# Maxout of the last three chunks as seven products of quarters, and a new order table

## The chip, the cores and the metric

The program runs on one core of a Trainium2 chip. The metric is the device time in microseconds (us) of one execution; lower is better. The engines are TensorE (PE in the profile, its weight loads PEld), VectorE (DVE), ScalarE (ACT), GpSimd (POOL) and SyncE (SP, which only issues DMAs here).

## What is computed

Linear attention with an exponential feature map over 8 batches of 8 heads, 576 positions and 64 channels, then a feed-forward layer whose hidden value is the maximum of three products (maxout):

```python
def phi(x):
    proj = np.einsum('bhsd,df->bhsf', x, w_phi)
    proj = proj - np.max(np.abs(proj), axis=-1, keepdims=True)
    return np.concatenate([np.exp(proj), np.exp(-proj)], axis=-1)
q_p, k_p = (phi(q), phi(k))
kv = np.einsum('bhsf,bhsd->bhfd', k_p, v)
z = np.sum(k_p, axis=2)
num = np.einsum('bhsf,bhfd->bhsd', q_p, kv)
den = np.einsum('bhsf,bhf->bhs', q_p, z)[..., None] + 1e-06
attn_out = num / den
x = attn_out.transpose(0, 2, 1, 3).reshape(B * S, H * D)      # 4608 x 512
h = np.maximum(np.maximum(x @ w1, x @ w2), x @ w3)            # 4608 x 768
out = h @ w_out                                               # 4608 x 512
```

## The kernel before

**Attention in 16 units.** A unit is half a batch: four heads. Its k and q come by DMAs on POOL's queue (nodes Lk and Lq, lines 431 and 421) into one of four slots `qk_bf` in bf16, its v by SP (Lv, into one of four slots `raw`). The channel-major copy `qkT` is made on PE for the first four units and by transposing DMAs of SP (T, line 516) for the others. PE projects (G, into `psk`, `pst`, `psq`; M, into `psm`), DVE takes the maxima (line 538), ACT the exponentials `Ek` and `Eq` (lines 542 and 622), POOL scales v into `vab` (line 586), PE sums `kvps` (K, line 605) and multiplies the numerators `psn` (N, line 672), DVE combines two halves into `y` (lines 681, 684) with a reciprocal (line 729), POOL divides (line 730), and a transposing DMA (X, line 762) puts the result into `xT`, four tiles of 128 channels by tokens.

**Feed-forward in nine chunks of 512 tokens.** Chunks 0 to 7 are the first 512 positions of a batch each; chunk 8 is the last 64 positions of all batches, gathered by POOL (C, lines 1044 and 1045). The maximum is taken relative to the first product: w2 and w3 are replaced by the differences w2−w1 and w3−w1 (line 976, six POOL instructions), and w1·w_out is one matrix, `line_w`. A chunk is then

out = x·(w1·w_out) + max(0, x·(w2−w1), x·(w3−w1))·w_out.

Per chunk PE makes 12 products of 128 hidden rows by 512 tokens (`up` and `up2`, line 880, four matmuls of 512 columns each into a PSUM bank `ups`). ACT or DVE cuts the first at zero into `hT` (lines 894, 896), DVE takes the maximum with the second (line 890). Then, for four tiles of 128 tokens, PE adds x·(w1·w_out) (`straight`, line 913) and hT·w_out (`down`, line 918) in one bank; ACT or DVE copies it (osb, line 928) and SP stores it.

**The order is a table.** The nodes are built in a fixed sequence and numbered; the text `PLAN` lists them again in the order in which they are emitted. A word such as `471G@74.8` is node 471 on engine G (T is PE, D is DVE, A is ACT, G is POOL, S is SP); digits before the @ are the slots or PSUM banks that it opens. Each engine does its nodes in that order and waits by semaphores for what a node needs. The number behind the @ orders nothing; the kernel only uses it in `fill`, which puts matmuls on a constant tile (`idler`, line 1060) where PE is expected to be free in the first 30 us.

**What is already there for the change.** `seven_products` and a block that makes `w_sums` exist before, but the set `SEVEN` of the chunks that use them is empty. For a pair jp of hidden blocks, with the chunk's x cut into quarters (halves of its tokens by halves of its channels) and both differences cut into halves of their channels, seven products of 256 tokens (`product`, each two blocks of two matmuls of 256 columns) give what eight give directly. They need sums of x quarters (`sums`, node xs, four per chunk) and of weight quarters (`w_sums`, node ws, four per pair). Behind each chain of products stand additions of a PSUM bank to a part in SBUF (`joined`, node uj, seven per pair, DVE), one copy (us, ACT), two cuts at zero (hr, ACT) and two maxima (hx, DVE). These temporaries take slots of others: `w_sums` all four of `qk_bf`, `sums` one of `qkT`, the parts two of `raw` per pair.

Of the kernel before, what the change touches and what calls it, by code (L numbers as in the profile page):

```python
# [55 lines left out]
SEVEN = ()  # L56
# [34 lines left out]
10S0@0.7 103G0@1.2 3S@1.1 1D@0.8 4A@1.1 5D@4.1 11A1@3.9 12D@4.3 0G@1.9 19T0@4.7 20D0@5.2 6A@4.2 29T12@5.6 34A0@6.1 32D0@6.1 33A0@6.5  # L91
9G@2.5 16S0@1.7 106T3@6.1 107D1@6.8 112T45@7.5 35D@7.3 119T67@7.7 31A@7.0 30A@7.5 8G@3.2 25T0@8.2 115D1@8.0 125D@8.6 116A1@8.0
117A1@8.5 7D@9.2 26D@9.3 102G@3.9 259G2@4.6 1166G@5.3 2G@6.1 186G3@6.3 17G@9.1 13S@3.1 118D@9.7 23T3@10.2 51T21@10.6 73T05@10.8
260G@9.3 104G@10.1 1169G@10.3 15D@10.3 14D@10.5 52D0@11.0 53D@11.6 27T2@11.8 28D@12.2 114A@8.9 120A@9.4 113A@9.9 121A@10.4 122D@12.4
76A0@11.2 124A@11.7 74A@12.2 77A0@12.7 21T1@12.4 43T24@12.7 110T6@13.2 22D@13.0 46D@13.3 75A@13.1 36T51@13.5 24D@13.7 47D@14.0
334S1@3.5 18S1@4.9 39D@14.3 108T0@13.8 185G@11.0 111D@14.9 48T34@14.5 42D@15.1 1167G@11.8 45A@13.8 54A0@14.1 44A@14.3 123A@14.6
38A@15.1 37A@15.6 56G0@14.5 55G@15.6 49D@15.7 109D@16.3 68T62@15.3 69A@16.1 58A@16.5 60G@16.9 105S2@5.6 126T75@16.2 50D@16.9 130D1@17.5
129D@17.9 57G@18.0 61G@18.1 59G@18.3 40A@16.7 70A@17.2 402G1@19.4 71A@17.7 41A@18.2 72A@18.7 134T30@17.1 136D@18.2 135D@18.8 62T45@18.3
78T6@18.9 137A1@19.1 81A0@19.3 79A@19.5 128A@19.8 131T12@19.3 64D0@19.4 63D@19.6 132D@19.8 187S0@10.4 80A@20.1 65T03@19.6 66D@20.4
151T54@20.1 82T16@20.6 67A@20.3 127A@20.5 141A@20.7 133D@20.6 90T03@20.9 83D0@21.2 155A1@20.9 154A1@21.4 91D1@21.6 85T72@21.4 86D@22.0  # L100
84D@22.4 92D@22.8 153A@21.9 1178T1@21.8 1180T4@22.2 93T07@22.7 1176T6@23.0 1179A0@22.4 152A@23.3 1181D@23.2 87D@23.8 161T3@23.4
138G1@20.1 190T1@23.5 162A@23.8 163A@24.1 191A2@24.3 1177D@24.2 94D@24.7 140G@21.2 142G@21.3 261G@22.4 139G@22.6 143G@23.7 1168G@24.8
144G@25.6 145T54@24.1 156T23@24.7 164A1@25.2 147A1@25.4 158A@25.6 157A@26.0 160A@26.5 88D0@25.1 95D@25.3 267T1@25.4 268D3@25.7
146D@25.9 265T6@25.5 148T04@26.1 404G@25.7 89G0@25.9 188G@27.1 96D1@26.1 97G@27.4 333G0@28.6 335G@29.3 337S0@40.7 332G@29.5 266D@26.2
165T27@26.7 168T15@27.1 150A@27.0 159A@27.1 149A@27.6 166D2@27.3 169D@27.7 194T6@27.5 263T4@27.6 167D@28.1 195A@27.9 173T30@28.1
196T21@28.5 170D@28.5 264A@28.3 176T76@28.9 174D0@28.9 171D2@29.3 177D@29.4 178D@30.0 175D@30.4 1186T5@29.2 200A0@29.2 201A0@29.7
198A@30.2 1187A@30.7 202D0@30.8 179D0@31.4 403G@30.3 172G1@31.0 203T43@30.6 276T76@30.8 180G@32.2 205A@31.1 208A@31.6 197A@32.1
280A1@32.6 281A1@33.0 207A@33.5 1172G@33.6 1170G@35.7 100T0@31.1 101D@31.6 279D1@32.0 192T5@31.4 189S3@42.1 193D@32.6 1184T1@31.9
1188T0@33.1 199D@33.2 282D@33.8 1185A@34.0 204A@34.5 283T52@34.5 262S0@42.8 181T6@34.7 1182T1@35.0 209D@34.4 287D0@35.0 206D@35.3
1171G@37.8 182D@35.9 1183D@36.5 277A@35.0 284A@35.4 1189A@35.7 278A@36.2 285A@36.6 183T3@36.3 301T24@36.7 184D@37.1 338S@43.5  # L110
473S0@45.0 405S1@46.9 336S2@47.6 1173G@39.9 1175G@42.0 98T6@37.0 99D@37.5 288T10@37.4 269T73@37.7 286D@37.9 290D@38.3 1202T6@38.1
302A0@37.1 304A@37.6 273A@38.1 751S1@48.2 303A0@38.6 305A@39.1 271A@39.6 1203A1@40.0 289D@38.9 291T50@39.0 406S1@49.6 274A@40.5
270A@41.0 1192T2@39.4 292D@39.5 293D@40.1 1193D@40.7 1198T4@40.2 1199D@41.3 210T61@41.2 213D@41.9 214D1@42.2 275D@42.6 228T50@41.3
1194T2@41.6 231A1@41.7 230A1@42.2 1195A@42.7 232A@43.2 1204T4@42.5 272D@43.2 1205D@43.8 1206T1@43.4 229A@43.6 306T32@44.3 218T07@44.5
1207D@44.4 219D@45.0 220D@45.6 215T45@44.8 1214T1@45.2 216D@46.2 1215D@46.8 1200T0@46.1 238T7@46.9 211A@44.1 221A0@44.4 309A@44.8
1196T4@47.0 310A@45.2 212A@45.7 294A1@46.0 308A@46.2 314A0@46.6 239A@47.2 307A@47.5 240A@48.0 217D@47.4 1201D@48.0 1174G@44.1
222G0@46.5 339T12@48.0 353T63@48.2 233T75@48.4 1197A@48.2 297A1@48.7 224A@48.8 357D0@48.6 223G@48.5 1212T0@48.8 356D0@49.0 345D@49.3
225T43@50.5 1213D@49.9 342D@50.5 236A@48.9 237A@49.4 234A@49.9 235A@50.4 241A1@50.9 295G@50.6 344A0@51.8 227D0@51.8 296G@52.7 226A@52.3
354A0@52.6 355A@52.8 343A@53.1 346T05@51.6 1210T7@51.9 242T34@52.8 407S@52.8 1208T6@53.2 541G2@54.7 352D@52.2 349D@52.8 243D1@53.4
1211D@53.8 752G3@55.4 472G0@55.7 749G@56.4 542G@57.1 351A@53.6 245T23@54.1 350A@54.0 341A@54.5 364A0@55.0 340A@55.2 298T75@54.7  # L120
244D@54.4 246D@54.8 1209D@55.2 415T14@55.8 247D@55.8 299A1@56.0 300A@56.3 348A@56.6 347A@57.0 418D1@56.3 250T26@56.2 253T37@56.5
1228T5@56.8 311T0@57.7 251D2@56.9 1216T2@57.8 254D@57.3 420A1@57.5 252D@57.7 255D@58.1 421D@58.5 365G0@57.8 313A@58.0 312A@58.2
# [170 lines left out]
def kernel(  # L293
# [798 lines left out]
```

## Time and profile before

| | |
|---|---|
| median of 3 timed runs | 283.32 us (283.1 to 283.32) |
| the profiled execution | 285.92 us, of it 284.1 us span |
| granted PE clock, mean | 0.988 |
| busy: PE, DVE, ACT, POOL | 269.6, 216.4, 200.8, 161.9 us |
| chain that ended last | PE 81%, DMA 7%, ACT 5%, DVE 3%, issue 2% |
| up matmuls (line 880) in that chain | 28% |

The span runs from the first to the last instruction; the execution's time has the launch around it as well. A row of the profile reads: line, engine, operation, output<-inputs with their shapes, count, then busy us and the mean duration of one in ns, then the idle time of that engine just before these instructions and what ended it. Matmul durations overlap, so how fast they follow each other is read from several in a row. The chain of work that ended last lists start, duration and what ran. In the table of stretches the busy us of each engine stand with the number of its instructions.

### The profile page before, as it was taken

The numbers are of one execution on the slowest core, as the hardware profiler recorded it, in microseconds if no ns is written. First come the engines' busy times: TensorE is split into PE (matmuls) and PEld (weight loads), VectorE is DVE, ScalarE is ACT, GpSimd is POOL, SyncE is SP. The second block draws the span as 40 slices with busy tenths as digits, with TensorE's granted clock in tenths as the row PEclk, the third lists the DMA queues.
The fourth block names the chain that finished last, engine by engine and source line by source line (L and its number), as shares of the span: only waits on it lengthen the run. The fifth ranks groups of instructions, "written<-read, shape, count | busy, mean of one in ns | idle before, by whom it ended". The sixth has DMA issues, their size and how long they took to land.

```text
span 284.1 us, 8392 instructions
## 1 busy us (share of the span) xinstructions
PE 269.6 (95%) x3399; PEld 151.8 (53%) x3438; DVE 216.4 (76%) x444; ACT 200.8 (71%) x482; POOL 161.9 (57%) x166
## 2 busy tenths in 40 slices
PE   6879999999996999999999999999999999999993
PEld 4647754576553465546654546555556654444442
DVE  2799999999895788999898898788997871055410
ACT  4599999999995789679889888689699320321011
POOL 8559999998496773462939716576764071000000
PEclk9799999999998999999999999999999999999999
DMA  7999999999999699999999697693027007040054
GB/s 135 244 229 205 208 187 253 260 194 187 224 144 193 129 236 145 218 229 189 254 186 181 143 196 163 160 211 60 3 77 131 2 3 200 2 178 6 3 140 155
DMA packets 76214, 44.52 MB, mean 157 GB/s; under 512 B 52688, under 2 KB 67344, under 8 KB 76176
## 3 DMA queue, kind: packets, MB, share of 16 engines
q1 hardware_dynamic: 61184, 32.19, 51.8%
q0 software_dynamic: 14912, 11.77, 27.9%
q8 instruction: 27, 0.44, 0.6%
q14 instruction: 11, 0.09, 0.1%
q10 hardware_dynamic: 80, 0.03, 0.0%
HBM read 34.64 MB, written 9.44 MB: 155 GB/s over the span
## 4 chain that ended last, share of the span: by engine, by line
PE 81%; DMA 7%; ACT 5%; DVE 3%; issue 2%; POOL 0%; POOLq 0%; ACTq 0%; DVEq 0%
PE ups L880 28%; PE ops L918 16%; PE ops L913 11%; PE psn L672 6%; PE kvps L605 6%; PE psk L534 3%; ACT Eq L622 2%; PE psm L631 2%; DMA qkT<-qk_bf 2%; PE psq L534 2%; DMA qk_bf<-in_q_dram 2%; DMA qk_bf<-in_k_dram 2%; PE pm L1012 2%; ACT Ek L542 1%; PE tps L497 1%
## 5 line engine op out<-in xcount | busy, mean ns | idle before, releaser
L880 PE MATMUL ups<-xT,w_bf 128*128 128x512 bf16 x415 | 101.6, 381 | 1.2 <-issue 0.2
L622 ACT ACTIVATE Eq<-psm 128x512 bf16<-128x512 f32 (+1 forms) x160 | 80.4, 575 | 11.4 <-PE psm L631 7.6
L586 POOL TENSOR_TENSOR vab<-v_raw,em 128x1152 bf16<-128x1152 f32 (+1 forms) x36 | 68.3, 1905 | 26.3 <-ACT em L580 25.1
L542 ACT ACTIVATE Ek<-psk 128x512 bf16<-128x512 f32 x128 | 71.4, 629 | 6.0 <-PE psk L534 5.0
L880 PEld LDWEIGHTS <-w_bf 128*128 128x128 bf16 x432 | 39.5, 98 | 43.5 <-issue 1.8
L730 POOL TENSOR_TENSOR x_sb<-y,rden 128x640 bf16<-128x640 f32 x32 | 39.8, 1254 | 35.8 <-DVE rden L729 28.5
L894 ACT ACTIVATE hT<-ups 128x512 bf16<-128x512 f32 x40 | 24.0, 611 | 37.9 <-PE ups L880 37.9
L918 PE MATMUL ops<-wout_bf,hT 128*128 128x512 bf16 (+2 forms) x215 | 50.2, 373 | 0.5 <-issue 0.2
L538 DVE TENSOR_REDUCE mk<-psk 128x4 f32<-128x512 f32 x64 | 42.8, 682 | 4.0 <-PE psk L534 2.3
L538 DVE TENSOR_REDUCE mq<-psq 128x4 f32<-128x512 f32 x64 | 41.5, 682 | 3.2 <-PE psq L534 3.0
L890 DVE TENSOR_TENSOR hT<-hT,ups 128x512 bf16<-128x512 bf16 x54 | 35.6, 675 | 9.9 <-PE ups L880 7.1
L681 DVE TENSOR_TENSOR y<-psn,sq 128x325 f32<-128x325 f32 x64 | 30.5, 490 | 9.9 <-PE psn L672 9.5
L918 PEld LDWEIGHTS <-hT 128*128 128x128 bf16 x222 | 20.6, 98 | 22.4 <-issue 0.2
L672 PEld LDWEIGHTS <-Eq 128*128 128x128 bf16 x640 | 26.4, 98 | 11.3 <-issue 0.9
L684 DVE TENSOR_TENSOR y<-y,psn 128x325 f32<-128x325 f32 x64 | 30.0, 487 | 2.4 <-DVE y L681 0.5
L672 PE MATMUL psn<-kv_sb,Eq 128*128 128x65 bf16 x640 | 28.8, 194 | 0.0
L928 ACT COPY osb<-ops 128x512 f32<-128x512 f32 (+2 forms) x25 | 14.6, 586 | 17.7 <-PE ops L918 13.1
L534 PEld LDWEIGHTS <-qkT 64*128 64x128 bf16 x576 | 18.4, 95 | 14.7 <-issue 10.9
L913 PE MATMUL ops<-xT 128*128 128x512 bf16 x85 | 24.2, 381 | 0.6
L605 PE MATMUL kvps<-vab,Ek 64*128 64x65 bf16 x1152 | 22.2, 191 | 0.2 <-POOL vab L590 0.2
L605 PEld LDWEIGHTS <-Ek 64*128 64x128 bf16 x1152 | 20.6, 94 | 2.3 <-DVE mk L538 0.4
L913 PEld LDWEIGHTS <-xT 128*128 128x128 bf16 x128 | 11.2, 98 | 12.7 <-issue 1.3
(68 smaller groups left out, 259.6 us busy)
## 6 DMA issues: line engine op xcount, KB each, us to landing
v_raw<-in_v_dram SPq DMA_DIRECT2D x16, 576.0 KB, 5.7
out_dram<-osb SPq DMA_DIRECT2D x32, 256.0 KB, 2.7
qk_bf<-in_k_dram POOLq DMA_DIRECT2D x15, 288.0 KB, 8.4
qk_bf<-in_q_dram POOLq DMA_DIRECT2D x15, 256.0 KB, 8.2
w_bf<-in_moe_w_dram POOLq DMA_DIRECT2D x3, 768.0 KB, 16.7
tail_raw<-in_q_dram SPq DMA_DIRECT2D x16, 64.0 KB, 5.6
wout_bf<-in_moe_w_out_dram POOLq DMA_DIRECT2D x1, 768.0 KB, 19.5
out_dram<-osb SPq DMA_DIRECT2D x6, 128.0 KB, 2.3
```

The lines of the kernel that those rows point to most:

```text
L534: nc.tensor.matmul(ps[s]()[:, i, :], lhsT=qkT()[r, n, :], rhs=wph[r, :], start=True, stop=True)
L538: return nd(kind, {"DVE": 0.598 if n == 4 else 0.331}, lambda: nc.vector.tensor_reduce(dst(m()), ps()[:, 0:n, :], AXX, ALU.max, apply_abso ...
L542: return nd("ek", {"ACT": 0.478 if n == 4 else 0.264}, lambda: nc.scalar.activation(dst(Ek[g]()), ps()[:, 0:n, :], EXP, scale=1.0 - 2.0 * ...
L586: made.append(chosen(n_, lambda n_, g=g, t0=t0, t1=t1: (nc.vector if n_.eng == "DVE" else nc.gpsimd).tensor_tensor(vab()[:, g, t0:t1, 0:D] ...
L605: nc.tensor.matmul(kvps[ab]()[:, pr, g, :], lhsT=Ek[g]()[r, t, :], rhs=vab()[r, g, t, :], start=(pr == prs[0] and g + j == 0), stop=(pr == ...
L622: return nd("eq", {"ACT": 0.478 if n == 4 else 0.264}, lambda: nc.scalar.activation(Eq[g]()[:, t0:t0 + n, :], ps()[:, 0:n, :], EXP, scale= ...
L672: nc.tensor.matmul(psn[g]()[:, i, :], lhsT=Eq[g]()[:, t, :], rhs=kv()[:, pr, ab, g, :], start=True, stop=True)
L730: divs[pr] = nd("x", {"POOL": 1.2}, lambda pr=pr, y=y, rden=rden: nc.gpsimd.tensor_tensor(x_sb()[:, pr].rearrange("p t a d -> p a t d"), y ...
L880: nc.tensor.matmul(ups()[:, o * n:(o + 1) * n], lhsT=w_bf[i + (not plain)][:, ct, jj * P:(jj + 1) * P], rhs=tokens_of(ct)[:, cols] if halv ...
L890: nc.vector.tensor_tensor(dst, dst, src, ALU.max)
L913: nc.tensor.matmul(ops_()[:, 0:hi - lo], lhsT=tile_of(ct, tt), rhs=line_w[c_i > MOVE][:, ct, lo:hi], start=(ct == 0), stop=False)
L918: nc.tensor.matmul(ops_()[:, 0:hi - lo], lhsT=hT()[:, j, tt * P:(tt + 1) * P], rhs=wout_bf[:, j, lo:hi], start=plain and j == 0, stop=(j = ...
```

## The change

Two edits in the code and a new table:

- `SEVEN` becomes chunks 6, 7 and 8: they use `seven_products` in place of 12 full products.
- The weight sums (ws) may stand on POOL only; before, DVE was named too. They did not exist in the program before, since `SEVEN` was empty.
- `PLAN` is replaced as a whole. It was laid out against five sets of measured DMA landings. With 1688 nodes instead of 1565, numbers from 1176 on are other nodes than before.

```diff
-SEVEN = ()
+SEVEN = (6, 7, 8)
...
 PLAN = """
-10S0@0.7 103G0@1.2 3S@1.1 1D@0.8 4A@1.1 5D@4.1 11A1@3.9 12D@4.3 0G@1.9 19T0@4.7 20D0@5.2 6A@4.2 29T12@5.6 34A0@6.1 32D0@6.1 33A0@6.5
...
+1560D@264.7 1668T@263.2 1669A0@264.7 1579D@265.0 1595T@264.5 1674S@258.6 1678S@261.9 1583T@265.8 1587T@267.1 1670S@265.4 1596D3@266.1
+1597S@266.8 1584A1@267.3 1588A2@268.6 1590T2@268.4 1591T@269.3 1585S@268.0 1589S@269.3 1592A0@270.8 1593S@271.4
...
-                got.append(chosen(node("ws", 0, {"DVE": 0.35, "POOL": 1.05}, None, need, used + [w_tiles[i]], port=True), minus_))
+                got.append(chosen(node("ws", 0, {"POOL": 1.05}, None, need, used + [w_tiles[i]], port=True), minus_))
```

The table has 11 more lines, so behind it a line of the kernel before, say 880, is line 891 after. What changes in the program, counted: PE has 288 up matmuls of 512 columns instead of 432, and 252 of 256 columns; DVE has 63 uj, 18 hx and 2 xs more, 18 maxima, 7 cuts at zero and 3 output copies less; ACT has 9 us and 18 hr more and 11 cuts less; POOL has 12 ws and 10 xs more. There are 63 idle matmuls instead of 48.

**POOL's queue at the loads of units 6 and 7.** L431 is a k load, L421 a q load, L586 and L590 make `vab`, L730 divides, L468 casts a piece of q's last positions. Before, the k load of unit 6 is followed by the q load of unit 10, then comes this stretch, from the k load of unit 7 to the q load of unit 6:

```order
L431 DMA qk_bf<-in_k_dram 128x2x576
L586 TENSOR_TENSOR vab<-v_raw,em 128x18x64
L590 CAST vab<-em 128x36
L468 CAST qk_bf<-tail_raw 128x2x64
L730 TENSOR_TENSOR x_sb<-y,rden 128x2x5x64
L586 TENSOR_TENSOR vab<-v_raw,em 128x18x64
L730 TENSOR_TENSOR x_sb<-y,rden 128x2x5x64
L468 CAST qk_bf<-tail_raw 128x2x64
L730 TENSOR_TENSOR x_sb<-y,rden 128x2x5x64 x2
L586 TENSOR_TENSOR vab<-v_raw,em 128x18x64
L590 CAST vab<-em 128x36
L421 DMA qk_bf<-in_q_dram 128x4x256
```

After (lines 11 higher), from the `vab` of unit 3 on: the k load of unit 6, the q loads of units 6 and 7, a division, the k load of unit 7:

```order
L597 TENSOR_TENSOR vab<-v_raw,em 128x18x64 x2
L442 DMA qk_bf<-in_k_dram 128x2x576
L432 DMA qk_bf<-in_q_dram 128x4x256 x2
L741 TENSOR_TENSOR x_sb<-y,rden 128x2x5x64
L442 DMA qk_bf<-in_k_dram 128x2x576
L601 CAST vab<-em 128x36
```

Unit 6's q load moved from behind its k load by twelve rows to directly behind it; unit 10's q load moved to a later place.

**DVE near the program's end.** Before, with `hT<-hT,ups` the maximum of the second product, `hT<-ups` the first cut at zero and `osb<-ops` an output copy, the last rows are:

```order
L890 TENSOR_TENSOR hT<-hT,ups 128x512 x3
L928 COPY osb<-ops 128x512
L896 TENSOR_SCALAR hT<-ups 128x512 x2
L890 TENSOR_TENSOR hT<-hT,ups 128x512
L896 TENSOR_SCALAR hT<-ups 128x512
L890 TENSOR_TENSOR hT<-hT,ups 128x512
L928 COPY osb<-ops 128x512
L896 TENSOR_SCALAR hT<-ups 128x512
L890 TENSOR_TENSOR hT<-hT,ups 128x512 x10
L928 COPY osb<-ops 128x512 x4
```

After, L829 is a join (uj), L864 an hx, L799 a sum of x quarters. A piece from the middle of the joins, where chunk 6 ends and chunks 7 and 8 begin:

```order
L829 TENSOR_TENSOR parts<-ups,parts 128x512 x3
L829 TENSOR_TENSOR hT<-ups,parts 128x2x256 x2
L829 TENSOR_TENSOR parts<-ups,parts 128x512
L829 TENSOR_TENSOR hT<-ups,parts 128x16x32
L799 TENSOR_TENSOR sums<-xT 128x512
L864 TENSOR_TENSOR hT<-hT,parts 128x2x256 x2
L829 TENSOR_TENSOR parts<-ups,parts 128x512 x3
L829 TENSOR_TENSOR hT<-ups,parts 128x16x32
L829 TENSOR_TENSOR parts<-ups,parts 128x512 x4
L864 TENSOR_TENSOR hT<-hT,parts 128x16x32 x2
```

DVE's last 27 instructions, behind its last reciprocal, become 80: 58 joins, 18 hx, one sum and three output copies.

**PE behind the last numerators.** Before, 120 matmuls of `ups` of 512 columns stand behind the last `psn`; after, 224 of 256 columns, with eight more of `straight` and six more of `down` (512 columns) that stood ahead of it. The last ten of all are, before, the 128 last columns of chunk 8, and after, a `straight` and a `down` of 512 columns of chunk 7.

More of the change, by code (lines that the diff above doesn't have):

```diff
@@ L95 @@
[L95 to L122, printed above, removed]
@@ new lines @@
+122D@10.6 26D@11.2 15D@11.5 117A@10.6 23T2@11.4 18S1@4.9 123A@11.1 116A@11.5 120A@12.0 24A@12.5 124A@13.0 1166G@11.0 188G@11.8
+1169G@12.0 51T10@11.8 115D@11.7 52D0@12.3 27T3@12.1 28D@12.9 14D@13.1 73T56@12.6 53D@13.3 74A0@13.4 105S2@5.6 1167G@12.7 75A0@13.9
+76A@14.4 77A@14.9 21T2@13.5 22D@13.9 43T74@13.8 48T13@13.9 46D@14.3 49D@14.6 47D@15.2 50D@15.5 54A0@15.3 68T05@14.6 36T62@15.5
+126T14@15.7 70A@15.6 44A@16.0 45A@16.3 69A@16.6 71A@17.0 72A@17.5 129D@16.1 42D@16.5 41A@18.0 333G1@13.9 334S0@9.0 108T3@16.3
@@ new lines @@
+1110T41@195.4 1117T57@195.6 1019D0@194.9 1020D@195.5 1405A@195.5 1115A@196.0 1412T2@195.8 1061G0@195.0 1060G@197.0 1416T3@196.7
+1420T0@197.5 1113D@195.9 1121D0@196.5 1116D@196.8 1120D@197.4 1417D@197.8 1111A@196.7 1062A@197.1 1413A@197.2 1118A@197.9 1119A@198.2
+1128A1@198.4 1129G1@199.1 1112A@198.6 1114A@199.1 1418T7@198.4 1021T32@199.2 1131G@201.2 1108A@199.6 1391S@182.0 1421D@198.6
+1424T5@199.6 1076T4@200.4 1078A0@200.7 1010T10@200.5 1022D@199.8 1419D@200.2 957S@193.3 1403S@195.1 1023D@200.8 1440T3@200.8
@@ new lines @@
+1011D@201.2 1107A@201.0 1071T72@201.8 1125T16@202.0 1024D0@201.6 1012D@201.8 1425D@202.2 1016D1@202.8 1441T@202.3 1436T0@203.7
+1025G1@201.9 1126D@202.9 1127D@203.5 1017G@203.1 1077A1@201.5 1072A@202.2 1074A@202.7 1075A@203.2 1073A@203.7 1442A3@204.2
+1122T51@204.6 1135T64@204.8 1053T27@205.1 1137A1@205.3 1136A0@205.7 1124D@205.1 1123D@205.6 1054D@206.2 1055D@206.8 1139A@206.2
+1399S@195.7 1138A@206.7 1145T3@205.3 1437T@205.5 1130G@204.3 1056T61@206.9 1146A@207.2 1602G@206.3 1026S@204.4 1132T52@207.1
@@ new lines @@
+1151D@212.7 1093D@213.1 1083T36@214.2 1472D@213.5 1470D1@214.1 1080T75@214.5 1450T4@214.8 1144A@213.4 1143A@213.9 1142A@214.4
+1141A@214.9 1433T@215.3 1160T01@216.6 1187G@213.9 1443S@205.9 1084D2@214.7 1155D2@215.1 1156G2@215.4 1081D@215.2 1085D@215.6
+1082D@216.0 1451D@216.4 1452T3@216.9 1486T7@217.3 1157T65@217.7 1094D0@217.0 1086D1@217.2 1161D1@217.3 1095G0@217.3 1604G@218.5
+1456T4@218.1 1434A0@216.8 1463A@217.2 1453D@217.7 1158D@218.3 1490T0@218.5 1459T2@218.9 1162D@218.7 1159D@219.1 1435S@217.4
@@ new lines @@
+1524G@236.5 1623T2@236.2 1530D@236.5 1624D@237.1 1535D0@237.7 1619D@238.3 1506T@236.7 1531T0@238.0 1527T5@238.4 1626D@238.9 1514T@238.8
+1515A1@240.3 1628D@239.2 1532D@239.6 1536T2@240.1 1528D1@240.3 1537D@240.9 1635T1@240.6 1629T3@241.0 1538T0@241.4 1534D@241.6
+1539D@242.2 1633T5@241.9 1631T2@242.3 1630A2@241.6 1634D@242.8 1632D@243.3 1636D3@243.9 1640T6@242.7 1637T0@243.2 1639D@244.5
+1648T3@243.6 1652T5@244.1 1650T2@244.5 1507A0@242.1 1644A@244.1 1540A@244.6 1649A0@245.1 1638D@245.1 1641D@245.7 1642T1@244.9
@@ new lines @@
+1659T4@245.3 1654T3@245.8 1671T0@246.2 1563T6@247.1 1653D@246.3 1643D@246.9 1646A@246.5 1564A3@247.7 1647D@247.5 1645D@247.9
+1655D2@248.2 1651D@248.8 1519A2@248.2 1520S@248.9 1660D@249.4 1665A@250.2 1663A@250.7 1667T5@247.5 1569T1@248.4 1656T6@248.8
+1661T3@249.2 1571T2@249.7 1582T7@250.1 1544T4@251.0 1658D@250.0 1657D@250.6 1662D@251.2 1664D@252.0 1666D@252.3 1567T6@251.4
+1679T3@252.0 1545A2@252.0 1565T4@252.6 1672T@253.1 1516S@249.5 1431S@250.1 1568D@252.7 1573D0@253.5 1570D@254.1 1542A@252.5 1543D@254.7
@@ new lines @@
+1566D@255.0 1680T@254.4 1578A@255.8 1681D2@255.6 1683T6@255.3 1548T1@255.6 1550T4@256.0 1684T@256.4 1673A1@256.2 1682S@256.2
+1508S@257.4 1572D@256.1 1541D@256.7 1594T3@256.8 1549D@257.0 1685D3@257.6 1686S@258.0 1551D1@257.8 1574T0@257.6 1552T2@258.1
+1546T1@258.5 1575D@258.4 1580A@259.2 1675T6@258.9 1676T@259.8 1557T4@261.1 1555T0@261.5 1687A@259.6 1677A2@261.3 1554D@259.0
+1547D@259.6 1553D@260.4 1556D@262.2 1561A@262.9 1559A@263.4 1558D@262.8 1581D@263.4 1562D@263.7 1586T6@261.9 1576T1@262.8 1577D@264.1
```

228 lines of the change are left out of this document (119 added, 109 removed).

## The prediction

> **What bounds the kernel now.** I read the engines' shares over the span first, then a table of five stretches, then the chain that ended last, and last the one wait in it that is not TensorE's.
>
> ```profile
> span 284.1 us, 8392 instructions
> ...
> PE   6879999999996999999999999999999999999993
> ...
> DVE  2799999999895788999898898788997871055410
> ACT  4599999999995789679889888689699320321011
> ...
> PEclk9799999999998999999999999999999999999999
> ```
>
> TensorE (PE) is full from the fourth slice to the end but for slice 13; VectorE (DVE) is nearly as full up to slice 32 and then half idle. The same by stretches (columns after the times: busy us of PE, PEld, DVE, ACT, POOL, then granted clock, DMA share, GB/s):
>
> ```profile
> 15.00:75.00 60.00, 58.09 (x969) 36.24 (x977) 58.92 (x128) 58.60 (x153) 52.77 (x49) 1.00 1.17 210
> 75.00:100.00 25.00, 22.04 (x275) 11.51 (x278) 18.89 (x40) 19.62 (x47) 20.37 (x22) 0.93 0.97 180
> 100.00:225.00 125.00, 123.68 (x1798) 70.42 (x1814) 108.49 (x222) 104.73 (x253) 72.58 (x67) 1.00 0.82 157
> 229.00:279.00 50.00, 49.74 (x231) 22.95 (x235) 19.78 (x33) 8.25 (x15) 4.73 (x6) 1.00 0.30 86
> ```
>
> Up to 75 us three engines share the limit. From 100 us PE sets the pace (1.3 us of 125 idle), and from 229 us it does so alone: DVE has 30.2 us of 50 free. The one hole is in 75 to 100, where PE has 3 us without work at a clock of 0.93. The chain there, and PE's own rows:
>
> ```profile
> 77.24 6.55 DMA qk_bf<-in_q_dram
> ...
> 83.81 6.95 DMA qkT<-qk_bf
> ...
> 90.80 0.61 PE psm L631
> ```
> ```profile
> 90.80 0.61 PE L631 MATMUL psm<-qkT,wph 64*128 64x512 bf16 x2 [2.64 <-DMA qkT<-qk_bf]
> ```
> ```profile
> 88.00:90.80 2.80, 0.17 (x6) 0.04 (x2) 1.06 (x2) 0.60 (x2) 0.68 (x1) 0.91 1.30 238
> 90.80:94.20 3.40, 3.18 (x18) 1.58 (x20) 1.21 (x3) 2.07 (x4) 3.29 (x4) 0.57 0.93 180
> ```
>
> GpSimd issues unit 6's q load at 77.24, it lands at 83.79, SyncE's transpose of it lands at 90.76, and PE waits 2.64 us. Then the clock is 0.57 for 3.4 us: at full clock its 3.4 us would have been 1.94, so 1.46 us more. **The stall costs 4.1 us in this execution.** The Trainium skill, "TensorE: Matmul & The Clock Gate", section "HAM oscillation — how this bites in real kernels", has only idle gaps above about 3.4 us throttle the clock; the 2.64 us here was followed by the low clock, so the trace does not agree.
>
> The sum starts from this execution's 285.92 us (span 284.1 and 1.8 outside it). The timed runs' median is 283.32, 2.6 less. PE's other rows are back to back, so I put that difference on the stall (my inference): about 1.5 of its 4.1 us is in the median.
>
> **The seven products: −3.5 us of PE.** The pitch of matmuls comes from the chain, where they stand back to back:
>
> ```profile
> 34.46 0.45 PE tps L497 x8
> ...
> 142.86 1.73 PE ups L880 x8
> ...
> 228.28 0.62 PE psn L672 x20
> 229.17 4.05 PE ups L880 x18
> ...
> 279.53 0.35 PE ops L918 x6
> ```
>
> 512 columns: 1.73/8 = 0.2163 us; 128 columns: 0.45/8 = 0.0562. On the line through both, 256 columns take 0.1096. Each of the three chunks gives up 48 matmuls of 512 (2 differences, 6 blocks, 4 channel tiles) for 84 of 256 (3 pairs, 7 products, 4 matmuls). That is 144 × 0.2163 = 31.1 us out, 252 × 0.1096 = 27.6 in: **−3.5**. Were 256 columns exactly half of 512, it would be −3.9; that end goes into the range. Weight loads double per column but are hidden beside matmuls (PEld 23 of 50 us).
>
> **Where it falls.** Behind the last psn matmul (numerators of the last unit) before has by the order 120 up matmuls and the rest of the down and straight ones, 51.1 us at these pitches; the chain has 228.90 to 279.88, 51.0. After, 224 of 256 columns (24.6 us), 120 of 512 (26.0), 10 of 384 (1.6) and 10 of 128 (0.6) stand there: 52.7. So 1.6 us more lies behind it, and 3.5 + 1.6 = 5.1 us less ahead. The attention ahead must then run 5.1 us tighter on DVE and ScalarE (ACT), which are 87% and 84% busy at 100 to 225. What PE loses in such company: 1% there now, 3.2% at 15 to 75 with both at 98%. On 125 us the range is 0 to 4.0 us more; I take **+1.4**, a loss twice today's, since the nearer row is this stretch's own.
>
> **Can DVE carry the joins?** It gets 63 joins (uj, a product in PSUM plus a part in SBUF), 18 hx (maximum of two bf16 halves in SBUF) and 2 of the token sums, and loses 18 maxima (L890), 7 of the first copies (L896) and three output copies on balance.
>
> ```profile
> L538 DVE TENSOR_REDUCE mk<-psk 128x4 f32<-128x512 f32 x64 | 42.8, 682 | 4.0 <-PE psk L534 2.3 <-ACT Ek L542 1.6
> ...
> L890 DVE TENSOR_TENSOR hT<-hT,ups 128x512 bf16<-128x512 bf16 x54 | 35.6, 675 | 9.9 <-PE ups L880 7.1 <-ACT hT L894 2.2 <-ACT sq L650 0.2
> ...
> L896 DVE TENSOR_SCALAR hT<-ups 128x512 bf16<-128x512 f32 x14 | 9.5, 685 | 10.7 <-PE ups L880 10.7
> ...
> L453 DVE CAST qk_bf<-k_raw 128x256 bf16<-128x256 f32 x1 | 0.3, 286 | 0.0
> ```
> ```profile
> 41.26 2.40 DVE mq L538 x4
> ```
>
> A DVE row of 512 values out of PSUM lasts 0.68 but its successor starts 0.60 after it (2.40/4). So a join is 0.60, or 0.68 where it is held until the one before is through. An hx has no row. It is at most the 0.60 of a PSUM operand; nearest is the cast within SBUF, 256 values in 0.286, less the 0.08 of overlap, twice: 0.41, taken. The lower end is that cast's own 0.286. By the Trainium skill, "VectorE: DVE Perf Modes", section "The perf-mode tier table (the rule you actually need)", two bf16 operands in SBUF run at twice the rate and a PSUM operand at the single one; with 256 cycles at the page's 0.96 GHz and its 58 fixed ones I estimate 0.33 for hx, which would shorten the DVE path below by 1.4 us and leave the forecast. No run here shows it yet.
>
> Behind DVE's last reciprocal stand 58 joins (34.8 us), 18 hx (7.4), a token sum (0.4) and three output copies (1.3): 43.9. That reciprocal was done 2.6 us after the last psn matmul:
>
> ```profile
> 231.51 0.22 DVE L729 RECIPROCAL rden<-y 128x10 f32<-128x10 f32 x1
> ```
>
> (231.51 less 228.90). Behind the last hx PE still has 22 matmuls of 512, 4.8 us. DVE's path is 2.6 + 43.9 + 4.8 = 51.3 against PE's 52.7: it fits with 1.4 us to spare, cost **0**, and it is the next bound.
>
> **GpSimd (POOL).**
>
> ```profile
> L976 POOL TENSOR_TENSOR w_bf<-w_bf 128x1024 bf16<-128x1024 bf16 x6 | 12.5, 2115 | 0.0
> ```
>
> Half of such a row, 1.06 us, times 12 weight sums and 10 token sums is 23 us. At 100 to 225 POOL has 52 us free, at 229 to 279 45: cost 0. Without that cover it would be the sum that a product waits for, 1.06 us each. The 9 copies and 18 relus on ACT come where it has 42 of 50 us free; the cost is 0 for the same reason. Bounds for both: 0 to 2 us, two late sums.
>
> **The stall.** After the change unit 6's q load stands directly behind its k load on POOL, no longer behind twelve rows of other work. In the trace that k load is issued at 58.25, the q load 19 us later:
>
> ```profile
> 58.25 0.70 POOL L431 DMA_DIRECT2D qk_bf<-in_k_dram x1
> ```
>
> So this wait goes. What is late next is open, since every load moves: transposes take 4.3 us in the middle and 7.2 at worst, tails 5.6, and some will stand as close to their users.
>
> ```profile
> qkT<-qk_bf SPq DMA_TRANSPOSE x24, 4.3
> ```
>
> Left over: 0 to 4.1; I take 0.9. Against the execution −3.2, against the median −0.6.
>
> **The end.** Before closes on 128 columns (ACT copy 265 ns); after on 512 (604 ns), with a store of 256 KB (2.7 us to land, against 2.2 to 2.5 of the small ones).
>
> ```profile
> L928 ACT COPY osb<-ops 128x512 f32<-128x512 f32 x23 | 13.9, 604 | 11.9 <-PE ops L918 7.4 <-DMA out_dram<-osb 4.5
> ...
> L928 ACT COPY osb<-ops 128x128 f32<-128x128 f32 x1 | 0.3, 265 | 0.0
> ```
> ```profile
> out_dram<-osb SPq DMA_DIRECT2D x32, 256.0 KB, 2.7
> ```
>
> 0.34 + 0.2 to 0.5, less the second queue's issue that falls away: **+0.4**, between 0 and 0.8. More idle fillers and moved loads in the first 15 us lie beside DMA waits: 0, within 0.5 either way.
>
> Sum: 285.92 − 3.5 + 1.4 + 0.4 − 3.2 = 281.0; from the median, 283.32 − 3.5 + 1.4 + 0.4 − 0.6 = **281.0**.
>
> **Rivals.**
> - *The joins are held* (slower). They read what a join before them wrote (u2, then u3, then c22). If each starts only when its predecessor is through, 58 × 0.08 = 4.6 us more, less the 1.4 spare: 281.0 + 3.2 = 284.2. It passes 283.9 from a join of 0.674 on. For it: chains of three in each pair; against: three pairs interleaved in the order. 0.13.
> - *Attention was the bound after all* (the change doesn't bring what it says). DVE and ACT keep the last psn matmul where it is, the 5.1 us become idle PE, and 1.6 more stands behind: 283.32 + 1.6 + 0.4 − 0.6 = 284.7; it passes 283.9 once 4.3 us are given back ahead. For it the 98% at 15 to 75, against it the 87% later. 0.08.
> - *A new late load.* A stall like the old one, 4.1 instead of 0.9: 284.2; a wait of 2.64 without the low clock 282.7. By the clock section of the Trainium skill above such a wait costs no more than itself. For it: all loads are moved, and the weight sums take the q/k buffers while units 12 to 15 still load; against: the DMA share falls to 0.82 after 100 us. 0.12.
> - *Nothing is given back.* 283.32 − 3.5 or 3.9, no stall (−1.5), +0.4: 278.3 to 278.7. 0.12.
>
> **How the numbers follow.** Forecast 280 to 282.5, chance 0.55; the rivals as above. Below 279.0 lies about 0.08 and above 284.2 about 0.11, so the range is 279.0 to 284.2. A measurement of this kernel tells about 0.2% from no change, 282.75 to 283.9. Faster: 0.55, 0.12 and 0.03 of the late load's low end, 0.70. Same: 0.05, 0.03 and 0.02 of the three others, 0.10. Slower: the rest, 0.20.
>
> **What would show it.** Right: 252 matmuls of 256 columns at a pitch of 0.11; no wait of PE on qkT above 1 us and the clock at 1.00 after the start; about 52.7 us from the last psn matmul to PE's end, PE above 98% there and DVE above 85%. Wrong: joins 0.68 apart and PE waiting for uj or hx (first rival); PE idle on DVE or ACT at 100 to 220 by more than 4 us (second); a DMA row as PE's longest wait, with a clock below 1 behind it (third).

## The result, and the profile after

The changed kernel took 280.43 us (median of 6 runs, 279.96 to 280.98), the kernel before beside it 283.21 us (6 runs, 281.7 to 286.17): ratio 0.9916, 95% interval 0.9891 to 0.994. Forecast were 281.0, between 279.0 and 284.2. The profiled execution took 280.52 us, of it 278.7 us span, where before had 285.92 and 284.1. The 285.92 and the 286.17 are runs of before in a slower state that enter no ratio, and what only that profile of before shows, its stall at 88 us above all, need not stand in the median.

From the page of the changed kernel, its span and its slices of two engines and the clock:

```profile
span 278.7 us, 8796 instructions
...
PE   7989999999999989999999999999999998999993
...
DVE  3899999999999869879889998999889999999950
...
PEclk9999999999999999999999999999999999999999
```

The hole of before in slice 13 and its low clock are gone. DVE, which was mostly idle from slice 34 on, is now full up to slice 38. (The code is 11 lines longer, so line 880 of before is 891 now, 672 is 683, 918 is 929; the seven products are line 820. The other kernels below have tables of other lengths, so the same lines mostly carry other numbers there: the products are 812, joins 821, hx 856.)

The same by stretches (columns after the times: busy us of PE, PEld, DVE, ACT, POOL, then granted clock, DMA share, GB/s):

```profile
75.00:100.00 25.00, 23.98 (x357) 13.37 (x357) 22.36 (x46) 23.30 (x57) 18.92 (x19) 1.00 1.19 208
100.00:225.00 125.00, 124.92 (x1790) 72.30 (x1791) 111.13 (x231) 103.58 (x251) 91.93 (x85) 1.00 0.80 151
225.00:276.00 51.00, 48.67 (x326) 30.95 (x323) 43.00 (x76) 18.38 (x33) 9.15 (x9) 1.00 0.26 77
```

At 75 to 100 PE has 1.9 us more than before and the full clock. At 100 to 225 it is idle for 0.08 us. The 1.3 us that seemed idle there in before are hardly waiting: matmul records are missing there. Line 880 has 432 weight loads but 415 matmuls:

```profile
L880 PE MATMUL ups<-xT,w_bf 128*128 128x512 bf16 x415 | 101.6, 381 | 1.2 <-issue 0.2
L880 PEld LDWEIGHTS <-w_bf 128*128 128x128 bf16 x432 | 39.5, 98 | 43.5 <-issue 1.8
```

Where one is missing, the neighbours start 0.43 us apart, two pitches, and a gap of 0.05 us seems idle; 22 such gaps make 1.2 of the 1.3 us, and the one wait in the stretch is 0.2. The trace of before lacks 39 over the span, those of experiments 1 to 4 and 8 as many or 40, that of the changed kernel none; so between them waits are compared here, not busy time. DVE went up by 2.6 us in that stretch. PE's waits from 99 us on are two (who waited for whom, us in total, times, longest):

```profile
PE psk L545 <- DMA qkT<-qk_bf: 1.0, 1, 1.0
PE ops L929 <- DVE hT L864: 0.8, 1, 0.8
```

The second is new. PE waits for hx (line 864), the maximum of two bf16 halves on DVE. That group's row shows why: 18 instructions with a mean of 554 ns,

```profile
L864 DVE TENSOR_TENSOR hT<-hT,parts 128x512 bf16<-128x512 bf16 x18 | 9.3, 554 | 0.1
```

and all its instructions taken alone say that most take 416 ns and the longest 1380:

```profile
L864 DVE TENSOR_TENSOR hT<-hT,parts x18: 411/416/1380, 226.6 to 268.7; 128x512 bf16<-128x512 bf16 x18
```

The timeline around that wait (start, us, engine) shows what stands beside the long ones:

```profile
228.80 1.15 POOL L799 TENSOR_TENSOR sums<-xT 128x512 bf16<-128x512 bf16 x1
...
229.26 2.27 DVE L864 TENSOR_TENSOR hT<-hT,parts 128x512 bf16<-128x512 bf16 x2
...
230.03 1.22 POOL L799 TENSOR_TENSOR sums<-sums,xT 128x512 bf16<-128x512 bf16 x1
...
231.46 1.27 DVE L829 TENSOR_TENSOR parts<-ups,parts 128x512 f32<-128x512 f32 x2
...
231.59 1.04 PE L929 MATMUL ops<-wout_bf,hT 128*128 128x512 bf16 x4 [0.83 <-DVE hT L864]
```

GpSimd makes token sums there. The first hx ends at 230.23, 0.28 after the first sum (229.95), the second at 231.53, 0.28 after the second sum (231.25): 0.97 and 1.38 us for what takes 0.42 alone. Joins beside the third sum keep their pace (two in 1.27 us). The Trainium skill, "SBUF — State Buffer", section "Who interferes with whom", says that a DVE instruction with two inputs in SBUF contends with a GpSimd instruction that reads SBUF, and calls the port pair that they share an exclusive lock. The trace agrees: an hx has both inputs in SBUF and ends a fixed 0.28 us after the sum; a join has one in PSUM and is not held.

Behind the last psn matmul stand 54.2 us up to PE's end (220.33 to 274.52); in before it was 51.0, the forecast was 52.7. PE is busy for 98.4% of that stretch and DVE for 88%, as the prediction's signs ask.

### The profile page after: what moved, and what is told of

The parts are those of the page before. It is cut to its first block, busy times and chain, and to the rows that moved or that the text cites. A ratio compares the mean times of both kernels' runs of the same rounds, so it can differ in the third digit from the quotient of the medians.

```text
span 278.7 us, 8796 instructions
## 1 busy us (share of the span) xinstructions
PE 269.0 (97%) x3561; PEld 161.7 (58%) x3561; DVE 243.5 (87%) x497; ACT 212.9 (76%) x507; POOL 186.7 (67%) x184
## 4 chain that ended last, share of the span: by engine, by line
PE 83%; DVE 6%; ACT 4%; DMA 3%; issue 2%; POOL 1%; DVEq 0%; ACTq 0%; POOLq 0%
PE ups L891 23%; PE ops L929 15%; PE ops L924 10%; PE ups L820 7%; PE psn L683 7%; PE kvps L616 6%; PE psk L545 3%; PE psm L642 3%; DMA qkT<-qk_bf 3%; PE psq L545 3%; PE pm L1023 2%; ACT Ek L553 2%; DVE parts L829 2%; PE tps L508 1%; DVE hT L864 1%
## 5 line engine op out<-in xcount | busy, mean ns | idle before, releaser
L553 ACT ACTIVATE Ek<-psk 128x512 bf16<-128x512 f32 x128 | 72.5, 639 | 5.8 <-PE psk L545 5.3
L891 PE MATMUL ups<-xT,w_bf 128*128 128x512 bf16 x288 | 70.1, 379 | 0.0
L929 PE MATMUL ops<-wout_bf,hT 128*128 128x512 bf16 (+2 forms) x222 | 52.1, 373 | 0.8 <-DVE hT L864 0.8
L549 DVE TENSOR_REDUCE mq<-psq 128x4 f32<-128x512 f32 x64 | 40.9, 681 | 4.0 <-PE psq L545 3.6
L891 PEld LDWEIGHTS <-w_bf 128*128 128x128 bf16 x288 | 25.0, 98 | 26.8 <-issue 1.7
L939 ACT COPY osb<-ops 128x512 f32<-128x512 f32 x28 | 16.8, 599 | 20.5 <-PE ops L929 19.6
L829 DVE TENSOR_TENSOR parts<-ups,parts 128x512 f32<-128x512 f32 (+1 forms) x45 | 29.1, 679 | 0.5
L901 DVE TENSOR_TENSOR hT<-hT,ups 128x512 bf16<-128x512 bf16 x36 | 23.9, 681 | 1.4 <-PE ups L891 1.0
L862 ACT ACTIVATE hT<-hT 128x512 bf16<-128x512 bf16 x18 | 10.7, 625 | 18.5 <-DVE hT L829 18.5
```

The lines of the kernel that those rows point to most:

```text
L549: return nd(kind, {"DVE": 0.598 if n == 4 else 0.331}, lambda: nc.vector.tensor_reduce(dst(m()), ps()[:, 0:n, :], AXX, ALU.max, apply_abso ...
L553: return nd("ek", {"ACT": 0.478 if n == 4 else 0.264}, lambda: nc.scalar.activation(dst(Ek[g]()), ps()[:, 0:n, :], EXP, scale=1.0 - 2.0 * ...
L829: return ff("uj", {"DVE": 0.598}, lambda: nc.vector.tensor_tensor(runs(dst()) if dst not in own else dst(), runs(ps()), runs(src()), ALU.add),
L891: nc.tensor.matmul(ups()[:, o * n:(o + 1) * n], lhsT=w_bf[i + (not plain)][:, ct, jj * P:(jj + 1) * P], rhs=tokens_of(ct)[:, cols] if halv ...
L929: nc.tensor.matmul(ops_()[:, 0:hi - lo], lhsT=hT()[:, j, tt * P:(tt + 1) * P], rhs=wout_bf[:, j, lo:hi], start=plain and j == 0, stop=(j = ...
```

## The experiments

Nine experiments ran, in three series. Each is timed beside the kernel before on the same chip, so its ratio is to that. The kernel before itself was at 282.91 (23 runs; experiments 1 to 4), 282.04 (19; 5, 6 and 7) and 281.85 (11; 8 and the repetition of 6); its runs spread from 280.5 to 287.5.

**1. The stall of before, taken out alone.** Unit 6's q load moves up on POOL, the kernel is otherwise before's.

```diff
 472G0@55.7
+471G@74.8
 749G@56.4
...
-471G@74.8
 435G@75.5
```

> The kernel before, with one word of its table moved: the q load of unit 6 directly behind its k load. Theory (the stall at 88 us is this load landing late): PE's 2.6 us wait on qkT and the low clock behind it go, the time falls by 1.0 to 1.5 us from the median of before (283.2), to about 282, and by up to 4 where a run of before has the whole stall. Rival (all transposes wait for the same full DMA queues, the wait goes to another load): a wait of PE on a DMA of 1 us or more stands elsewhere and the time stays within 0.3 us of before.

282.63 us (281.75 to 283.67, 12 runs), ratio 1.0003 (0.9981 to 1.0024). In its profile the wait is gone:

```profile
75.00:100.00 25.00, 24.79 (x360) 13.75 (x362) 22.44 (x45) 23.39 (x58) 22.61 (x24) 1.00 1.07 195
```

PE has 2.75 us more in the stretch than in before's profiled execution, the span is 280.0 against 284.1, and yet the medians differ by 0.3 us only, against 1.0 to 1.5 expected. No wait of PE on a DMA above 0.5 us stands elsewhere, so the rival's other late load is not there either. So the stall belonged to some executions of the kernel before, its profiled one among them, and not to the one in the middle. The granted clock of the single runs agrees: 3.4 us at half clock alone would bring the mean over a run to 0.994, and 12 of the 23 runs of before have 0.997 or more.

**2. The stall put into the changed kernel.** Unit 6's q load goes behind the second scaling of v of unit 5, its transpose behind two stores.

```diff
 472G2@54.8
-471G@55.6
...
 435G@72.0
+471G@55.6
...
-477S@73.7
...
 1239S@78.9
+477S@73.7
```

> The changed kernel, with unit 6's q load put back behind the second vab of unit 5 and its transpose behind two stores, as the order before had them. Theory: PE waits 1.5 to 3 us on qkT near 90 us, with a clock below 1 behind it, and the time is 281.5 to 284.5 instead of 280.4. Rival (the new order has slack there by other moves): no wait of PE on qkT above 1 us, 280.4 within 0.3.

287.4 us (286.55 to 289.12), ratio 1.0171 (1.0138 to 1.0204): 7.0 us above the changed kernel, beyond the range of the theory. The chain of waits of its profile (start, us, what):

```profile
75.74 9.23 DMA qk_bf<-in_q_dram
...
84.98 6.96 DMA qkT<-qk_bf
...
91.99 0.61 PE psm L634 x2
```

The load issued at 75.74 lands after 9.23 us (6.55 in before), the transpose after 6.96, and PE waits 5.1 us, up to 91.99; the clock from 90 to 95 us is 0.66, which costs 1.7 us more. The two make 6.8 of the 7.0 us. So with the new table, too, this load must be early, and its place and its transpose's keep the wait away.

**3. All late token sums on DVE.** Seven sums of the last two chunks move from GpSimd to DVE in the changed kernel.

```diff
-1606G2@228.6
-1607G@229.7
-1608G@230.7
+1606D2@228.6
+1607D@229.7
+1608D@230.7
...
-1522G@233.3
+1522D@233.3
...
-1609G@234.4
-1523G@235.4
-1524G@236.5
+1609D@234.4
+1523D@235.4
+1524D@236.5
```

> The changed kernel, with the seven sums of x quarters of chunks 7 and 8 that stood on GpSimd moved to VectorE. Theory (GpSimd's sums of two bf16 tiles in SBUF slow the hx maxima beside them, three of which take 0.97 to 1.38 us instead of 0.42, and PE waits 0.8 to 1.3 us for them): all 18 hx take 0.42, VectorE gains about 2.5 us and pays 7 x 0.33 = 2.3, PE's wait at 230 us goes, 279.0 to 279.6. Rival (the sums cost as much on VectorE as they free): 280.4 within 0.3, or up to 1 us more.

280.38 us, ratio 0.9915 (0.9891 to 0.9939), the same as the changed kernel; 279.0 to 279.6 was expected. No hx is long any more (shortest, median and longest ns):

```profile
L856 DVE TENSOR_TENSOR hT<-hT,parts x18: 411/415/425, 226.2 to 268.4; 128x512 bf16<-128x512 bf16 x18
```

but PE now waits for a sum that stands behind a row of joins on DVE:

```profile
PE ups L812 <- DVE sums L791: 1.1, 2, 0.9
```

The contention is real and its removal by this way brings nothing: another wait takes its place.

**4. The new table alone.** The new order up to chunk 6; chunks 6 to 8 again as 12 full products each, in before's order, so without any weight or token sum.

```diff
-SEVEN = (6, 7, 8)
+SEVEN = ()
...
 PLAN = """
...
-1597S@266.8 1584A1@267.3 1588A2@268.6 1590T2@268.4 1591T@269.3 1585S@268.0 1589S@269.3 1592A0@270.8 1593S@271.4
+1561T@273.8 1511S@274.3 1562A1@274.3 1564A@274.7 1563S@274.9
```

> The new table up to chunk 6, but chunks 6 to 8 by twelve full products as before, in the order of before, and no weight sums or token sums (all is computed). Theory (the products are worth their PE columns, 3.5 us, less 1 to 2 us of waits for VectorE at the end): 282 to 284. Rival (the new order of loads is what gains, and VectorE at the end gives the products' gain back): 280 to 281.

282.1 us (12 runs), ratio 0.9971 (0.9949 to 0.9993). The table by itself is worth 0.8 us in this series, and the products on top of it 1.7 us by the medians (282.1 to 280.43; to experiment 3, in the same series, 1.72). The two profiled executions have 1.2 us between them (PE's end at 275.71 and 274.52). In experiment 4 the last psn matmul stands at 222.59 and in experiment 1 at 224.75, but ten more matmuls (250 for 240) stand behind it, and PE's end is 275.71 in both.

The single runs add something. Experiment 4 spreads from 281.65 to 282.75, before beside it from 280.54 to 284.62 without its slowest run: the table narrows the spread, and the fastest runs of before are faster than any of experiment 4. A mean granted clock below 0.996 stands in 26 of the 53 runs of before in the three series and in 7 of 12 of experiment 1, but in none of 12 here, and in one of the 44 of the other runs with the new table in which unit 6's load is early. That is not shown to be the 0.8 us, for the 12 runs of before in this series at 0.997 or more have a median of 282.9 as well.

**5. The products on the old table.** Before's order up to unit 15's transposes, behind it seven products in an order of my own. Against the changed kernel:

```diff
 PLAN = """
-1D@0.8 4A@1.1 103G0@1.2 10S0@0.7 3S@1.1 9G1@1.9 8G@2.6 2D@0.9 16S0@1.7 11A@3.9 12D@3.9 7D@4.1 5D@4.3 102G@3.4 0G@4.1 19T0@4.8 20D0@5.2
+10S0@0.7 103G0@1.2 3S@1.1 1D@0.8 4A@1.1 5D@4.1 11A1@3.9 12D@4.3 0G@1.9 19T0@4.7 20D0@5.2 6A@4.2
...
-1597S@266.8 1584A1@267.3 1588A2@268.6 1590T2@268.4 1591T@269.3 1585S@268.0 1589S@269.3 1592A0@270.8 1593S@271.4
+1587T@270.9 1584A2@271.1 1585S@271.7 1591T@272.1 1588A0@272.3 1589S@273.0 1592A3@273.6 1593S@274.3
```

> Before's table up to unit 15's transposes, so the old order of loads and of attention; behind it seven products in chunks 6 to 8 with the weight sums on GpSimd, in an order of my own that is planned about as well as the changed kernel's. Theory (the products are worth their 1.7 us on any table): 280.9 to 282.0, and 25 or more below 283.2 in hundredths for each chunk, that is 0.5 us for each of three. Rival (they pay only with the new order of attention, because DVE holds the rest): 282.5 to 284.5, with PE idle ahead of the last psn matmul by 4 us or more as in before (4.9) and 2 us or more behind it.

286.57 us, ratio 1.0142 (1.0096 to 1.0187): above both ranges of the expectation. PE's waits from 220 us on:

```profile
PE ups L812 <- DVE parts L821: 2.1, 2, 1.1
PE ups L812 <- DVE y L684: 1.1, 1, 1.1
```

PE is idle 3.45 us behind the last psn matmul (before has no wait there), and only 0.5 ahead of it, from 30 us on; the 4.9 that the expectation names for before are its stall of 2.64 and, for the most part, gaps of missing records. Behind these waits the clock is 0.51 from 234.2 to 237.7 us, 1.7 us more. So the rival had the side right but not the place: the loss lies where joins stand behind the last `y` on DVE. With a tail that is ordered worse the products lose more than they give. What the old order of attention would give with a good tail stays open, since only the tail of mine was tried.

**6. Four of the sums moved, away from the hx.** In the changed kernel chunk 8's first token sum and the last two of chunk 7 go to DVE, chunk 8's last one goes ahead of one of chunk 7, and the last transpose with its copies goes ahead on its queues.

```diff
 1096S@221.3
+1164G@220.5
+1165S@222.8
+1605G@227.8
+1606D2@228.6
...
-1164G@220.5
-1165S@222.8
-1605G@227.8
-1606G2@228.6
 1607G@229.7
...
+1609G@234.4
 1522G@233.3
...
-1609G@234.4
-1523G@235.4
-1524G@236.5
+1523D@235.4
+1524D@236.5
```

> The changed kernel with four of eight token sums of the last two chunks moved: the first sum of chunk 8 and the last two of chunk 7 from GpSimd to DVE, the last of chunk 8 ahead of one of chunk 7, and the last transpose and its copies ahead on their queues, so that no GpSimd sum lies beside an hx product and no sum is late. Theory (a GpSimd sum beside hx makes it 0.97 to 1.38 us instead of 0.42, and PE waits 0.85 us behind the last psn matmul for that and for nothing else): at most two of 18 hx above 0.5 us, PE idle at most 0.3 us behind the last psn matmul, 279.4 to 279.9. Rival (another wait takes its place at once, as with all seven sums on DVE): PE idle 0.8 us or more there, 280.2 to 280.7.

279.69 us (279.19 to 280.78, 8 runs), ratio 0.9905 (0.9871 to 0.994). One hx of 18 is still long:

```profile
L856 DVE TENSOR_TENSOR hT<-hT,parts x18: 414/419/1377, 227.0 to 268.6; 128x512 bf16<-128x512 bf16 x18
```

It meets the one sum left in the way, and PE is not waiting for it (PE idle 0.03 us behind the last psn matmul). From there to PE's end it is 53.7 us, 0.5 less than in the changed kernel. It ran once more:

> The kernel with four of the token sums moved, once more, to see whether its 0.7 us over the changed kernel hold: theory 279.4 to 280.0 with PE idle at most 0.3 us behind the last psn matmul; rival (the difference was the spread of the runs) 280.2 to 280.7.

279.71 us (279.1 to 280.64, 6 runs), ratio 0.9916 (0.989 to 0.9941), again with no wait of PE there. Beside the changed kernel of the next experiment the first is 0.67 us (0.24%) ahead. That is less than either spreads over, and both intervals overlap with the changed kernel's; twice 279.7 against 280.4 and 280.4 makes it the fastest by its median, not clearly so.

**7. The changed kernel again**, in the same series as experiment 5 and the first run of 6.

> The changed kernel unchanged, beside the other two on the same chip. Theory: 280.2 to 280.7, three hx above 0.9 us again and 54.0 to 54.4 us from the last psn matmul to PE's end, so that the profiled execution stands for the others. Rival (the three long hx were a chance of one execution): none or one above 0.9 us, 53.3 to 53.6 us behind the last psn matmul.

280.36 us (12 runs), ratio 0.9943 (0.9911 to 0.9975), hx of 0.94, 1.37 and 1.38 us at the same three places, 54.17 us behind the last psn matmul. The profile stands for the others. The gain over before is 0.84% in the first series and 0.57% in this one, with intervals that overlap.

**8. The weight sums on DVE.** The part of the change that names GpSimd alone is undone, the twelve sums stay at their places.

```diff
-                got.append(chosen(node("ws", 0, {"POOL": 1.05}, None, need, used + [w_tiles[i]], port=True), minus_))
+                got.append(chosen(node("ws", 0, {"DVE": 0.35, "POOL": 1.05}, None, need, used + [w_tiles[i]], port=True), minus_))
...
-1184G1@116.5
+1184D1@116.5
...
```

> The changed kernel with the twelve weight sums on DVE instead of GpSimd, at the same places of the order. On GpSimd they took 1.15 to 1.17 us each, 14 us together; on DVE they should take about 0.42 each like hx, 5 us together, in a stretch (116 to 217) where PE has no room and DVE about a tenth. Theory (GpSimd takes them at no cost, DVE is the tighter engine): 281.0 to 283.0, PE idle ahead of the last psn matmul 2 us or more against 1.0 to 1.4. Rival (where they stand makes no difference, or GpSimd's sums slow DVE's work beside them by as much): 280.0 to 280.8, PE idle ahead 1.5 us or less.

284.35 us (284.18 to 285.29), ratio 1.0084 (1.006 to 1.0108): 4 us above the changed kernel, above the kernel before, and past the theory's range. The stretch up to 225 us and PE's longest waits in it:

```profile
100.00:225.00 125.00, 120.75 (x1731) 69.56 (x1751) 114.58 (x236) 103.41 (x250) 76.38 (x71) 1.00 0.73 147
```
```profile
PE psn L675 <- DVE y L687: 1.0, 1, 1.0
PE ops L916 <- DVE mq L541: 0.9, 1, 0.9
PE psn L675 <- DVE osb L931: 0.4, 1, 0.4
```

All of PE's waits in that stretch make 3.1 us, and the last psn matmul slid from 220.33 to 223.83, 3.5 us. (The busy time fell by 4.2, from 124.92 to 120.75, but 1.1 of that are gaps of missing records.) DVE was busy for 92% of the stretch, 89% in the changed kernel. The sums took 9.0 us on DVE, not 5:

```profile
L993 DVE TENSOR_TENSOR w_sums<-w_bf 128x512 bf16<-128x512 bf16 x6 | 5.5, 915 | 0.0
L993 DVE TENSOR_TENSOR w_sums<-w_bf,w_sums 128x512 bf16<-128x512 bf16 x6 | 3.5, 586 | 0.0
```

Seven of the twelve take more than 0.42 us, and each of these ends 0.27 to 0.29 us after an instruction of GpSimd, as the long hx do.

## Why the prediction was right, and where it was not

**The products, −3.5: right in pace.** All 252 matmuls of 256 columns run; four in a row start 0.437 us after the four before them, 0.109 each against the 0.1096 of the line:

```profile
243.31 0.60 PE L820 MATMUL ups<-xT,w_sums 128*128 128x256 bf16 x4
243.75 0.60 PE L820 MATMUL ups<-sums,w_sums 128*128 128x256 bf16 x4
```

**The give-back, +1.4 ahead of the last psn matmul: near in size, by luck.** Of the forecast −3.5 + 1.4 + 0.4 = −1.7 for the products, 1.7 came by medians and 1.2 by profiled executions. But the step behind the 1.4 failed. It took the 1.3 us of idle time at 100 to 225 for what PE loses to full DVE and ACT, and doubled it; 1.2 of these were missing records. After the change PE is idle there for 0.08 us. Ahead of the last psn matmul PE waits 1.3 us from 30 us on, of them 1.0 for a transposed load at 99 us (0.6 in experiment 7), and 0.4 in experiment 4, without the products.

The larger loss stands behind the last psn matmul, where I had put 52.7 us with no wait and 54.2 were measured. Two things make up nearly all of the difference. One is the 0.83 us for the long hx. The other is joins: from 240 to 251 DVE has joins and hx in an unbroken row, each join 0.60 us, while PE makes a product in 0.437:

```profile
245.12 1.87 DVE L829 TENSOR_TENSOR parts<-ups,parts 128x512 bf16<-128x512 f32 x3
246.91 0.68 DVE L829 TENSOR_TENSOR hT<-ups,parts 128x512 bf16<-128x512 f32 x1
247.51 1.87 DVE L829 TENSOR_TENSOR parts<-ups,parts 128x512 f32<-128x512 f32 x3
...
253.75 1.87 DVE L829 TENSOR_TENSOR parts<-ups,parts 128x512 f32<-128x512 f32 x3
```
```profile
255.09 0.61 PE L820 MATMUL ups<-sums,w_sums 128*128 128x256 bf16 x4
255.68 0.81 PE L924 MATMUL ops<-w_bf,x_late 128*128 128x384 bf16 x4
```

From 255.09 to 255.68 PE took 0.59 us for a product: the next matmul stands behind the join that ends at 255.62. Six such holes between 246 and 256 us, each distance of two starts less the pitch, make 0.6 us. Five of them, 0.4 us, end with a join on DVE, and the largest, 0.19 us at 249.30, with ACT's copy of a product. 0.83 and 0.6 are 1.4 of the 1.5 us. I reckoned DVE's path as 51.3 against PE's 52.7 over the whole tail and called the cost 0; the spare was there in the sum and not in the place. That joins take 0.60 and are not held by their predecessors was right, and the rival of 0.68 apart fell. For the two profiled executions the sum closes: 3.5 less the 1.5 behind and the 0.9 more of waits ahead leaves 1.1, and PE's ends are 1.2 apart.

**GpSimd, 0: right for the weight sums, wrong for the token sums.** I asked whether GpSimd had time, and it had: undoing it costs 4 us (experiment 8). I did not ask what its sums do to DVE beside them. Two of the three long hx, one behind the other, cost PE 0.83, within the bound of 0 to 2 that I had set for another reason (a late sum). Experiment 6, which takes these two out of the way, removes the wait and gains 0.7 us by the medians; behind the last psn matmul it gains 0.5, for the holes behind joins grow from 0.6 to 1.1 us.

**hx, 0.41: its length, not its share of DVE's path.** 0.416 is the median length, but two in a row start 0.33 apart (two take 0.75). The path is added up from distances of starts, so the prediction's smaller estimate of 0.33 was the one to use. It makes the path shorter by up to 1.4 us and does not touch the forecast.

**The stall, −0.6 from the median: in size nearly what the table gave, by another cause.** I put 1.5 us of it in the median of before. Experiment 1 shows 0.3 there by the medians and at most 0.5 by the interval of the ratio. That the −0.6 still came near is luck. The table as a whole gave 0.8 (experiment 4, 0.2 to 1.4 by its interval), and what in it does so stays open: PE's end is the same in the profiles of experiments 1 and 4. The start, which I had put at 0, may have a part in it, since the clock differs between the tables and the new one has 15 more idle fillers; no run takes it apart. That the load no longer waits is right (PE's longest wait on `qkT` is 1.0 us, and no low clock follows), and that a late one is expensive is right and was priced too low: the rival of a late load had 3.2 us against the forecast, experiment 2 shows 7.

**The end, +0.4: not there.** From PE's end to the span's end it is 4.2 us in both (279.87 to 284.1, 274.52 to 278.7). Before had two copies and a second queue's store behind its small last piece, after has one:

```profile
279.39 0.82 ACT L928 COPY osb<-ops 128x512 f32<-128x512 f32 x2 [2.05 <-PE ops L918]
280.24 0.59 ACTq L932 DMA_DIRECT2D out_dram<-osb  x1
```
```profile
274.60 0.59 ACT L939 COPY osb<-ops 128x512 f32<-128x512 f32 x1 [1.57 <-PE ops L929]
275.21 0.33 SPq L943 DMA_DIRECT2D out_dram<-osb  x1
```

In sum, 281.0 was 0.6 above the measured 280.43: 0.4 of it is the end that was not there, the rest is within the spread. The pace of the products is the one large term whose mechanism held; the give-back and the stall came near for other reasons than those stated.

**The rivals.** Held joins and attention as the bound did not come; attention is near it, as experiment 8 shows, where 9 us of sums on DVE cost 4. No new late load came but the wait of 1.0 us at 99 us, with no low clock behind it. "Nothing is given back" would have been 278.3 to 278.7; the best order that ran stops at 279.7.

## What to carry to other kernels

Work that is moved from a full engine to a half-idle one has to fit in each stretch of some us, not in the sum over a stage: here DVE had 1.4 us to spare over 50 by the reckoning and yet held PE for 0.4 in ten. Where GpSimd takes over sums, ask which DVE instructions with two inputs in SBUF stand beside them, and set them apart, or leave on GpSimd only sums that meet none. A wait in one profiled execution is not yet a wait of the median: a kernel with that wait alone taken out tells them apart. And idle time that no wait accounts for is not a loss: compare the counts of matmuls and weight loads first.

## What the runs showed of the chip

- A DVE maximum of two bf16 tiles of 128x512 in SBUF takes 0.42 us; beside a GpSimd sum that reads SBUF it ends 0.28 us after that sum and so takes up to 1.38. Joins with one input in PSUM beside the same sums keep 0.60 us from start to start. With the sums gone all 18 take 0.411 to 0.425.
- A weight sum of the same shape took 1.15 to 1.17 us on GpSimd in the changed kernel, and 0.41 to 2.15 us on DVE in experiment 8, where the long ones end 0.27 to 0.29 us after an instruction of GpSimd.
- A q load issued late took 9.23 us to land (experiment 2), where the q loads of that kernel take 7.0 in the middle; with its transpose it cost 7 us of time for 5.1 us of waiting, with PE's clock at 0.66 from 90 to 95 us.
- One wait of PE of 2.64 us (before), and waits of 1.14 and 0.93 us within 2.7 us (experiment 5), were followed by a low clock (3.4 us at 0.57, and 3.5 us at 0.51); single waits of 1.0 and 0.83 us (changed kernel) were not.
